# Rotary attention and soft mixture of experts on one core: one normalising product per head pair, and values loaded ahead of weights

## The chip, the cores and the metric

The kernel runs on one core of a Trainium2 chip, in one launch. The metric is the device time in microseconds (us), the median of several runs. The core's engines are TensorE (PE, with its weight loads PEld), VectorE (DVE), ScalarE (ACT), GpSimd (POOL) and SyncE (SP), which here only issues transfers (DMAs).

## The reference

For 8 batches of 8 heads (576 positions, head size 64) queries and keys are rotated, and softmax attention is formed; its result, as 4608 rows of 512, then goes through a soft mixture of 8 experts with 4 slots each.

```python
q_rot, k_rot = (rotate(q), rotate(k))
scores = scale * np.matmul(q_rot, k_rot.transpose(0, 1, 3, 2))
scores = scores - np.max(scores, axis=-1, keepdims=True)
attn = np.exp(scores)
attn = attn / (np.sum(attn, axis=-1, keepdims=True) + 1e-09)
x = (attn @ v) as (B*S, H*D)
logits = x @ phi                       # 4608 x 32
d = softmax of logits over the rows;   slot_input = d.T @ x
slot_out[e] = relu(slot_input[e] @ w1[e]) @ w2[e]
c = softmax of logits over the slots;  out = c @ slot_out
```

## The kernel before

Attention is done for 32 pairs of heads, numbered 0 to 31, four to a batch. For a pair p, queries and keys come in as `x_in` (2 buffers), POOL multiplies them by cosines and sines in eight pieces (`spin0`, `spin1`, L213, called "spins" below), DVE adds the products (`join`, L217), ACT casts the sum to a high half (`high`, L222), and DVE subtracts that half to get the low one (`low`, L226: a subtraction with two inputs in the on-chip memory SBUF, from which POOL reads too). TensorE makes scores once for the row maxima (`m_unit`, L260, reduced on DVE in L262; `m_rem` L269 and L271), then once more from high and low halves with the maxima added (`score`, L313; `score_rest`, L328). The maxima travel from DVE (`m_min` L280, `m_turn` L286) through ACT (`m_half` L290) and five small transfers into `peak` (`m_rows`, L297 and L298). ACT takes the exponentials (L314, L332), and TensorE multiplies them with the values `v_in` (`av`, L344; `load_v`, L232, 2 buffers, so pair p takes the buffer of pair p-2).

`o_out` (ACT, L370 and L372) copies the unnormalised result to `o_sb`: five blocks of 128 positions a head, the fifth with 64 of 128 partitions. `recip` (DVE) adds 1e-9 to the sums, in two instructions L381 and L382, and inverts them (L383); `norm` (POOL) multiplies, in two instructions: L391 on 128 partitions and four blocks, L393 on 64 partitions and the fifth. `natural` (TensorE, L417) transposes the outcome for the logits.

The order of all this is written out by hand: a table gives each step a number (`WHEN`, the same in each pair, and `EARLY` for single steps of single pairs), steps are issued in the order of these numbers, and each engine and SP's queue work through theirs in order. SP's queue waits at its head: a transfer that may not start yet holds all behind it.

The experts' weights (64 tiles `w_exp` of 512 KB) are loaded partly during the last pairs, into space that the input buffers leave free after the last `low`. So that they don't all start at once, the table `PACE` names steps after which one or two such loads stand; each has a one-element memset on DVE ahead (L590), on which the transfer waits, so it can't start before DVE has got that far. The last of them is paced by a one-element copy on POOL instead (L593), which reads the weight tile loaded two earlier. The remaining weights follow when the last pair is done, and stream in while the experts' products (L855, L876) run.

The change touches `PACE`, two numbers of `EARLY` and the functions `o_out`, `recip` and `norm`.

Of the kernel before, what the change touches and what calls it, by code (L numbers as in the profile page):

```python
# [7 lines left out]
F32 = mybir.dt.float32  # L8
# [3 lines left out]
ALU = mybir.AluOpType  # L12
# [21 lines left out]
N_O = 2  # L34
# [15 lines left out]
VW = 66  # L50
N_HL = 3
N_XN = 1
WIDE = True
PACE = {("low", 30): 2, ("recip", 28): 1, ("m_min", 31): 1, ("av0", 30): 1, ("m_rows", 31): 1, ("av0", 31): 1}
WHEN = {
# [70 lines left out]
    30): 122.656032, ("load_v", 30): 122.656033, ("av0", 30): 124.276322, ("norm", 29): 124.926062, ("m_turn",  # L126
# [16 lines left out]
def attn_softmoe(ctx, tc, qk, v, phi, w1, w2, cs, ident, sel, seg, out):  # L143
    nc = tc.nc
    P = 128
# [9 lines left out]
    att = trans.enter_context(tc.tile_pool(name="att", bufs=1))  # L155
# [91 lines left out]
    def free(t):  # L247
        k, _ = held.pop(id(t))
        age[k] = next(ages)
# [86 lines left out]
    os_ = {}  # L336
# [25 lines left out]
    xn_sb = [xp.tile([P, 5, DM], F32, name=f"xn{i}") for i in range(N_XN)]  # L362
    for t in xn_sb:
        nc.gpsimd.memset(t[64:P, 4], 0.0)
    osb = {}

    def o_out(p):
        osb[p] = t = att.tile([P, 2, 5, VW], F32, name="o_sb", bufs=N_O)
        o = os_.pop(p)
        nc.scalar.copy(out=t.rearrange("p h u x -> p h (u x)")[:, :, 0:4 * VW], in_=o[:, :, 0:4 * VW])  # L370
        for h in range(2):
            nc.scalar.copy(out=t[0:64, h, 4], in_=o[rows[h], h, 4 * VW:5 * VW])  # L372
        free(o)

    rrs = [const.tile([P, 2, 5], F32, name=f"rr{i}") for i in range(2)]
    for t in rrs:
        nc.gpsimd.memset(t, 1.0)

    def recip(p):
        rr, t = rrs[p % 2], osb[p]  # L380
        nc.vector.tensor_scalar_add(out=rr[:, :, 0:4], in0=t[:, :, 0:4, 64], scalar1=1e-9)  # L381
        nc.vector.tensor_scalar_add(out=rr[0:64, :, 4], in0=t[0:64, :, 4, 64], scalar1=1e-9)  # L382
        nc.vector.reciprocal(out=rr, in_=rr)  # L383

    def norm(p, eng):
        b, pp = divmod(p, NP)
        if pp == 0:
            xns[b] = xn_sb[b % N_XN]
        xn = xns[b][:, :, pp * P:(pp + 1) * P].rearrange("p j (h x) -> p h j x", h=2)
        t, rr = osb.pop(p), rrs[p % 2]  # L390
        eng.tensor_tensor(out=xn[:, :, 0:4], in0=t[:, :, 0:4, 0:64],  # L391
                          in1=rr[:, :, 0:4].unsqueeze(3).broadcast_to([P, 2, 4, 64]), op=ALU.mult)
        eng.tensor_tensor(out=xn[0:64, :, 4], in0=t[0:64, :, 4, 0:64],  # L393
                          in1=rr[0:64, :, 4].unsqueeze(2).broadcast_to([64, 2, 64]), op=ALU.mult)

    def norm_last(p):
        t = os_.pop(p)
# [207 lines left out]
    def trickle(p, eng=nc.vector):  # L605
        if later:
            load_w(*later.pop(0), pace=eng)
# [135 lines left out]
    for when, n, q in events:  # L743
        run(n, q)
        if n == "low":
            lows.discard(q)
            if not lows and not extra:
                release_io()
        for _ in range(PACE.get((n, q), 0)):
            trickle(last, nc.gpsimd if n == "load_v" else nc.vector)  # L750
# [9 lines left out]
    p = last  # L760
# [21 lines left out]
    m, al, dt, xn = state["m"], state["al"], state["dt"], xns.pop(B - 1)  # L782
# [30 lines left out]
    for i in range(NP):  # L813
# [8 lines left out]
                            in1=e.unsqueeze(1).broadcast_to([P, NP, NS]), op=ALU.mult)  # L822
# [19 lines left out]
    for _ in range(N_LEAD):  # L842
        load_w(wp, N_W)
    nc.vector.tensor_tensor(out=st[:, :, 0:NS], in0=fp[:, 0:P].rearrange("p (c n) -> p c n", c=NP),
                            in1=zw.unsqueeze(1).broadcast_to([P, NP, NS]), op=ALU.mult)
# [166 lines left out]
```

## Time and profile before

| what | value |
|---|---|
| time, median of 3 runs | 524.99 us (521.03, 525.75, 524.99) |
| the profiled execution: its time, and its span | 519.47 us, 517.7 us |
| busy: PE, DVE, ACT, POOL | 473.2, 390.8, 300.8, 296.5 us |
| mean granted TensorE clock | 0.969 of full speed |
| chain that ended last | PE 66%, DVE 25%, issue 3%, DMA 3% |
| one pair of heads, in the middle | about 12 us |
| attention ends, experts begin | about 450 us |
| transfers | 94.03 MB, 182 GB/s in the mean |

The profile shows one execution. Its time and its span differ by 1.8 us, which lie around the instructions. TensorE is busy nearly all the time, so what counts is where it is not, and where its clock falls. The granted clock is given as a share of 2.4 GHz; 0.5 is the lower level, 1.2 GHz. In a list of instructions in order of time, a row has its start, its length, engine, line, operation, what it writes and reads, and in brackets the idle time of the engine ahead of it with what ended it. SPq rows are transfers being issued, not their duration. Several like instructions are merged into a row, with their count after an x.

### The profile page before, as it was taken

How to read it: one execution, taken by the hardware profiler on the slowest of the kernel's cores; microseconds unless marked ns; L12 is line 12 of the kernel's file. 1: busy time of each engine (PE TensorE's matmuls, PEld its weight loads, DVE VectorE, ACT ScalarE, POOL GpSimd, SP SyncE). 2: the span in 40 equal slices, each digit the busy share in tenths (PEclk: the TensorE clock that was granted, in tenths of full speed). 3: DMA queues.
4: the chain of work that ended last, by engine and by line, in shares of the span. 5: the costliest groups of instructions: out<-in, count | busy, mean ns of one | idle time of the engine just before them, and what ended most of it. 6: DMA issues, size and time to landing. Idle time of an engine off the chain costs nothing.

```text
span 517.7 us, 23365 instructions
## 1 busy us (share of the span) xinstructions
PE 473.2 (91%) x10320; PEld 372.5 (72%) x10320; DVE 390.8 (75%) x654; ACT 300.8 (58%) x674; POOL 296.5 (57%) x350
## 2 busy tenths in 40 slices
PE   4499999999999999999999999999969996989990
PEld 2278888787877878787878777878748886843650
DVE  5999988888878887888788878888877851342271
ACT  2156666566666666666766676667637751762551
POOL 2969987577758775867687767728564210220000
PEclk9699999999999999999999999999979997999996
DMA  7267464334544454444444444435322035299998
GB/s 259 92 206 247 165 212 174 124 141 166 217 188 154 161 172 152 163 161 161 162 161 161 162 162 162 161 96 187 120 73 74 5 126 175 91 390 409 395 355 328
DMA packets 29509, 94.03 MB, mean 182 GB/s; under 512 B 5088, under 2 KB 6880, under 8 KB 29408
## 3 DMA queue, kind: packets, MB, share of 16 engines
q1 hardware_dynamic: 29388, 92.54, 49.0%
q8 instruction: 81, 1.33, 1.0%
q14 instruction: 20, 0.16, 0.1%
q10 hardware_dynamic: 20, 0.00, 0.0%
HBM read 83.02 MB, written 9.44 MB: 179 GB/s over the span
## 4 chain that ended last, share of the span: by engine, by line
PE 66%; DVE 25%; issue 3%; DMA 3%; ACT 1%; SPq 0%; POOL 0%; DVEq 0%; ACTq 0%
PE s_ps L313 21%; PE s_ps L344 18%; DVE nm L262 8%; DVE hl L226 6%; PE s_ps L260 5%; DVE x_in L217 5%; PE s_ps L328 4%; PE s_ps L417 4%; PE o_ps L876 3%; PE sp_ps L855 3%; DVE rr L381 2%; PE s_ps L436 2%; PE s_ps L492 1%; DMA out<-w_exp 1%; PE c_ps L902 1%
## 5 line engine op out<-in xcount | busy, mean ns | idle before, releaser
L213 POOL TENSOR_TENSOR x_in<-x_in,cs_sb 128x288 f32<-128x288 f32 x248 | 223.2, 935 | 74.5 <-DMA x_in<-in_qk 73.0
L262 DVE TENSOR_REDUCE nm<-s_ps 128x2 f32<-128x576 f32 x256 | 185.7, 748 | 48.0 <-PE s_ps L260 44.5
L314 ACT ACTIVATE a_t<-s_ps 128x576 f32<-128x576 f32 x256 | 146.7, 655 | 9.8 <-PE s_ps L313 7.9
L344 PE MATMUL s_ps<-v_in,a_t 128*64 128x66 f32 x4608 | 146.8, 224 | 5.7 <-DMA v_in<-in_v 4.4
L344 PEld LDWEIGHTS s_ps<-v_in,a_t 128*64 128x64 f32 x4608 | 141.0, 139 | 15.3 <-issue 7.7
L313 PE MATMUL s_ps<-hl 64*128 64x288 f16 x1536 | 132.0, 284 | 0.0
L313 PEld LDWEIGHTS <-hl 64*128 64x128 f16 x1536 | 78.2, 94 | 17.0 <-issue 2.4
L370 ACT COPY o_sb<-s_ps 128x528 f32<-128x528 f32 x31 | 18.6, 600 | 98.8 <-PE s_ps L344 91.6
L313 PE MATMUL s_ps<-peak,lift 64*128 64x288 f16 x512 | 74.1, 284 | 0.0
L260 PE MATMUL s_ps<-hl 64*128 64x288 f16 x512 | 64.5, 289 | 7.3 <-ACT hl L222 4.1
L222 ACT CAST hl<-x_in 128x576 f16<-128x576 f32 (+1 forms) x66 | 40.9, 655 | 38.6 <-DVE x_in L217 38.5
L391 POOL TENSOR_TENSOR xn<-o_sb,rr 128x512 f32<-128x512 f32 x31 | 41.3, 1331 | 30.2 <-issue 25.1
L226 DVE TENSOR_TENSOR hl<-x_in,hl 128x1152 f16<-128x1152 f32 x32 | 58.0, 1812 | 0.5 <-ACT hl L222 0.5
L217 DVE TENSOR_TENSOR x_in<-x_in 128x1152 f32<-128x1152 f32 (+2 forms) x36 | 51.0, 1419 | 0.4 <-issue 0.3
L260 PEld LDWEIGHTS <-hl 64*128 64x128 f16 x512 | 25.4, 94 | 20.6 <-issue 10.0
L313 PEld LDWEIGHTS <-lift 64*128 64x128 f16 x512 | 25.6, 94 | 6.0
L328 PE MATMUL s_ps<-hl 64*64 64x320 f16 (+1 forms) x384 | 21.7, 292 | 9.0 <-DVE nm L262 8.8
L344 PEld LDWEIGHTS s_ps<-v_in,a_tr 64*64 64x64 f32 x1152 | 21.9, 133 | 10.2 <-issue 10.0
L381 DVE TENSOR_SCALAR rr<-o_sb 128x8 f32<-128x8 f32 x31 | 18.1, 583 | 11.1 <-ACT o_sb L370 11.0
L344 PE MATMUL s_ps<-v_in,a_tr 64*64 64x66 f32 x1152 | 26.4, 224 | 0.0
L271 DVE TENSOR_REDUCE nm<-s_ps 128x2 f32<-128x576 f32 x32 | 23.9, 748 | 2.8 <-PE s_ps L269 2.8
L332 ACT ACTIVATE a_tr<-s_ps 128x512 f32<-128x512 f32 x32 | 19.1, 598 | 10.4 <-PE s_ps L328 9.6
(167 smaller groups left out, 451.2 us busy)
## 6 DMA issues: line engine op xcount, KB each, us to landing
x_in<-in_qk SPq DMA_DIRECT2D x62, 576.0 KB
w_exp<-in_w SPq DMA_DIRECT2D x63, 512.0 KB
v_in<-in_v SPq DMA_DIRECT2D x32, 330.0 KB
out<-w_exp SPq DMA_DIRECT2D x18, 512.0 KB
peak<-mr SPq DMA_DIRECT2D x126, 0.5 KB
x_in<-in_qk SPq DMA_DIRECT2D x4, 288.0 KB
cs_sb<-in_cs SPq DMA_DIRECT2D x2, 288.0 KB
peak<-mr SPq DMA_DIRECT2D x32, 0.2 KB
```

The costliest lines, as they stand in the source:

```text
L213: eng.tensor_tensor(out=x[:, :, c], in0=x[:, :, c], in1=cs_sb[:, :, c], op=ALU.mult)
L217: nc.vector.tensor_tensor(out=x[:, t, 0, c], in0=x[:, t, 0, c], in1=x[:, t, 1, c], op=ALU.add)
L222: nc.scalar.copy(out=halves[p][:, 1 + t, c], in_=loaded[p][:, t, 0, c])
L226: nc.vector.tensor_tensor(out=hl[:, 0:4:3], in0=x[:, :, 0], in1=hl[:, 1:3], op=ALU.subtract)
L260: nc.tensor.matmul(s[c, h, 0:HC], lhsT=hl[rows[h], QH, P * j + c.start:P * j + c.stop], rhs=hl[rows[h], KH, half[n]], start=True, stop=True)
L262: nc.vector.tensor_reduce(out=nm[:, n, j:8:4], in_=s[:, :, 0:HC], axis=AX.X, op=ALU.max, negate=True)
L313: nc.tensor.matmul(s[c, h, 0:HC], lhsT=lhs, rhs=rhs, start=(x == 0), stop=(x == 3))
L314: nc.scalar.activation(out=ats[p, b][:, :, half[n]], in_=s[:, :, 0:HC], func=AF.Exp, scale=SCALE)
L328: nc.tensor.matmul(s[rows[h ^ n], n, 0:w] if n else s[rows[h], 0, 512 - w:512], lhsT=lhs, rhs=rhs, start=(x == 0), stop=(x == 3))
L344: nc.tensor.matmul(o[rows[c], h, VW * u:VW * u + VW], lhsT=lhs, rhs=v, start=(i == 0 and u == first), stop=stop)
L381: nc.vector.tensor_scalar_add(out=rr[:, :, 0:4], in0=t[:, :, 0:4, 64], scalar1=1e-9)
L391: eng.tensor_tensor(out=xn[:, :, 0:4], in0=t[:, :, 0:4, 0:64], in1=rr[:, :, 0:4].unsqueeze(3).broadcast_to([P, 2, 4, 64]), op=ALU.mult)
```

## The change

`o_sb` becomes two fixed tiles, whose lower half of the fifth block (partitions 64 to 127) is set to zero once. `recip` then adds 1e-9 to all ten sums in one instruction, and `norm` is one POOL instruction over 128 partitions and five blocks; the rows that don't exist are products with zero. In the table, `load_v` of pairs 30 and 31 gets smaller numbers, and the weight load that stood after `m_min` of pair 31 now stands after `m_rows` of pair 31, which has two.

```diff
-PACE = {("low", 30): 2, ("recip", 28): 1, ("m_min", 31): 1, ("av0", 30): 1, ("m_rows", 31): 1, ("av0", 31): 1}
+PACE = {("low", 30): 2, ("recip", 28): 1, ("av0", 30): 1, ("m_rows", 31): 2, ("av0", 31): 1}
...
-    30): 122.656032, ("load_v", 30): 122.656033, ("av0", 30): 124.276322, ("norm", 29): 124.926062, ("m_turn",
+    30): 122.656032, ("load_v", 30): 115.540001, ("av0", 30): 124.276322, ("norm", 29): 124.926062, ("m_turn",
...
-    31): 126.278278, ("av1", 30): 126.278280, ("m_rows", 31): 126.373682, ("av4", 30): 127.875064, ("o_out",
+    31): 116.602001, ("av1", 30): 126.278280, ("m_rows", 31): 126.373682, ("av4", 30): 127.875064, ("o_out",
...
-    osb = {}
+    o_sbs = [att.tile([P, 2, 5, VW], F32, name=f"o_sb{i}") for i in range(N_O)]
+    for t in o_sbs:
+        nc.gpsimd.memset(t[64:P, :, 4], 0.0)
...
     rrs = [const.tile([P, 2, 5], F32, name=f"rr{i}") for i in range(2)]
-    for t in rrs:
-        nc.gpsimd.memset(t, 1.0)
...
-        rr, t = rrs[p % 2], osb[p]
-        nc.vector.tensor_scalar_add(out=rr[:, :, 0:4], in0=t[:, :, 0:4, 64], scalar1=1e-9)
-        nc.vector.tensor_scalar_add(out=rr[0:64, :, 4], in0=t[0:64, :, 4, 64], scalar1=1e-9)
+        rr, t = rrs[p % 2], o_sbs[p % N_O]
+        nc.vector.tensor_scalar_add(out=rr, in0=t[:, :, :, 64], scalar1=1e-9)
         nc.vector.reciprocal(out=rr, in_=rr)
...
-        t, rr = osb.pop(p), rrs[p % 2]
-        eng.tensor_tensor(out=xn[:, :, 0:4], in0=t[:, :, 0:4, 0:64],
-                          in1=rr[:, :, 0:4].unsqueeze(3).broadcast_to([P, 2, 4, 64]), op=ALU.mult)
-        eng.tensor_tensor(out=xn[0:64, :, 4], in0=t[0:64, :, 4, 0:64],
-                          in1=rr[0:64, :, 4].unsqueeze(2).broadcast_to([64, 2, 64]), op=ALU.mult)
+        t, rr = o_sbs[p % N_O], rrs[p % 2]
+        eng.tensor_tensor(out=xn, in0=t[:, :, :, 0:64], in1=rr.unsqueeze(3).broadcast_to([P, 2, 5, 64]), op=ALU.mult)
```

SP's queue near the end of attention, from the small transfers of pair 30 (`peak_105`) to those of pair 31 (`peak_106`) and the paced weights (`w_exp`); the two `v_in` are the values of pairs 30 and 31. Before:

```order
L297 DMA peak_105<-mr 2x4x32 x4
L298 DMA peak_105<-mr 2x2x32
L594 DMA w_exp<-in_w 128x1024 x4
L232 DMA v_in<-in_v 128x660
L594 DMA w_exp<-in_w 128x1024
L232 DMA v_in<-in_v 128x660
L297 DMA peak_106<-mr 2x4x32 x4
L298 DMA peak_106<-mr 2x2x32
L594 DMA w_exp<-in_w 128x1024 x2
```

And after:

```order
L297 DMA peak_105<-mr 2x4x32 x4
L298 DMA peak_105<-mr 2x2x32
L232 DMA v_in<-in_v 128x660
L589 DMA w_exp<-in_w 128x1024 x2
L232 DMA v_in<-in_v 128x660
L589 DMA w_exp<-in_w 128x1024 x2
L297 DMA peak_106<-mr 2x4x32 x4
L298 DMA peak_106<-mr 2x2x32
L589 DMA w_exp<-in_w 128x1024 x3
```

The values of pair 30 moved from behind four weights to ahead of all of them, those of pair 31 from behind five to behind two, and one weight from ahead of `peak_106` to behind it.

DVE at the same place: the last reductions of the maxima of pair 31, their minimum (`min_122`) and turn, and the memsets that release paced weights. Before:

```order
L262 TENSOR_REDUCE nm_8890<-s_ps_9261 128x2
L262 TENSOR_REDUCE nm_8890<-s_ps_9286 128x2
L280 TENSOR_REDUCE min_122<-nm_8890 128x9
L590 MEMSET w_exp 1x1 x2
L286 STREAM_TRANSPOSE turned<-min_122 128x32
L590 MEMSET w_exp 1x1
L518 TENSOR_REDUCE cm<-ln 128x5
```

And after:

```order
L262 TENSOR_REDUCE nm_8807<-s_ps_9178 128x2
L262 TENSOR_REDUCE nm_8807<-s_ps_9203 128x2
L280 TENSOR_REDUCE min_122<-nm_8807 128x9
L585 MEMSET w_exp 1x1
L286 STREAM_TRANSPOSE turned<-min_122 128x32
L585 MEMSET w_exp 1x1 x2
L513 TENSOR_REDUCE cm<-ln 128x5
```

One of the two memsets between the minimum and its turn moved behind the turn.

POOL around the normalisation of pair 25, which stands ahead of twelve spins. Before:

```order
L514 TENSOR_TENSOR ln<-ln,cm 128x160
L213 TENSOR_TENSOR x_in<-x_in,cs_sb 128x2x144 x4
L391 TENSOR_TENSOR xn_125<-o_sb,rr_128 128x2x4x64
L393 TENSOR_TENSOR xn_125<-o_sb,rr_128 64x128
L213 TENSOR_TENSOR x_in<-x_in,cs_sb 128x2x144 x12
L391 TENSOR_TENSOR xn_125<-o_sb,rr_127 128x2x4x64
L393 TENSOR_TENSOR xn_125<-o_sb,rr_127 64x128
```

And after:

```order
L509 TENSOR_TENSOR ln<-ln,cm 128x160
L213 TENSOR_TENSOR x_in<-x_in,cs_sb 128x2x144 x4
L389 TENSOR_TENSOR xn_125<-o_sb_128,rr_132 128x2x5x64
L213 TENSOR_TENSOR x_in<-x_in,cs_sb 128x2x144 x12
L389 TENSOR_TENSOR xn_125<-o_sb_127,rr_131 128x2x5x64
```

Of each two products one is left, and the spins that follow stand right behind it. The order on TensorE and ScalarE is the same in both kernels.

## Rows read from the trace of the kernel before

**Rows 1.** Whom TensorE waited for: us in total, times, longest us
```profile
PE s_ps L328 <- DVE nm L262: 8.8, 11, 5.1
...
PE s_ps L344 <- DMA v_in<-in_v: 4.4, 1, 4.4
```

**Rows 2.** SP's queue in order of time, 416 to 432 us: start, us, line
```profile
416.81 11.30 SPq L594 DMA_DIRECT2D w_exp<-in_w  x4
428.20 0.38 SPq L232 DMA_DIRECT2D v_in<-in_v  x1
...
429.63 2.16 SPq L297 DMA_DIRECT2D peak<-mr  x4
431.84 0.51 SPq L298 DMA_DIRECT2D peak<-mr  x1
```

**Rows 3.** The chain that ended last, in order of time: start, us, what
```profile
427.56 0.18 DVE min L280
...
428.20 3.71 DMA v_in<-in_v
...
432.05 7.68 PE s_ps L344 x177
...
444.77 5.12 PE s_ps L344 x180
```

**Rows 4.** Stretches: PE, PEld, DVE, ACT, POOL busy, granted clock, DMA share, GB/s
```profile
371.88:390.39 18.51, 13.41 (x283) 10.79 (x284) 15.58 (x19) 7.90 (x17) 10.47 (x14) 0.82 0.16 52
390.39:402.22 11.83, 11.78 (x287) 10.31 (x286) 8.34 (x15) 8.09 (x19) 5.57 (x6) 1.00 0.27 83
...
432.05:439.00 6.95, 6.95 (x145) 6.88 (x146) 0.00 (x0) 0.00 (x0) 0.00 (x0) 0.60 0.53 186
444.70:449.06 4.36, 4.36 (x146) 4.29 (x144) 1.49 (x5) 2.30 (x6) 0.91 (x2) 1.00 0.18 68
...
456.00:489.00 33.00, 32.52 (x358) 15.52 (x360) 8.98 (x26) 15.59 (x38) 3.99 (x9) 1.00 1.02 405
```

**Rows 5.** DVE in order of time around 373 us
```profile
372.71 0.17 DVE L381 TENSOR_SCALAR rr<-o_sb 128x8 f32<-128x8 f32 x1
...
372.98 0.22 DVE L383 RECIPROCAL rr<-rr 128x10 f32<-128x10 f32 x1
...
374.39 7.58 DVE L226 TENSOR_TENSOR hl<-x_in,hl 128x1152 f16<-128x1152 f32 x1
```

**Rows 6.** POOL in order of time around 373 us
```profile
373.34 1.04 POOL L391 TENSOR_TENSOR xn<-o_sb,rr 128x512 f32<-128x512 f32 x1 [2.83 <-DVE rr L383]
374.35 0.40 POOL L393 TENSOR_TENSOR xn<-o_sb,rr 64x128 f32<-64x128 f32 x1
374.70 6.05 POOL L213 TENSOR_TENSOR x_in<-x_in,cs_sb 128x288 f32<-128x288 f32 x8
```

**Rows 7.** All instructions of line 226: ns least/median/most, first and last start
```profile
L226 DVE TENSOR_TENSOR hl<-x_in,hl x32: 1317/1578/7583, 11.7 to 415.0; 128x1152 f16<-128x1152 f32 x32
```

**Rows 8.** DVE and POOL in order of time in two other pairs
```profile
113.85 1.57 DVE L226 TENSOR_TENSOR hl<-x_in,hl 128x1152 f16<-128x1152 f32 x1
...
113.80 0.40 POOL L393 TENSOR_TENSOR xn<-o_sb,rr 64x128 f32<-64x128 f32 x1
...
322.86 2.20 DVE L226 TENSOR_TENSOR hl<-x_in,hl 128x1152 f16<-128x1152 f32 x1
...
322.80 1.04 POOL L391 TENSOR_TENSOR xn<-o_sb,rr 128x512 f32<-128x512 f32 x1
323.80 1.51 POOL L393 TENSOR_TENSOR xn<-o_sb,rr 64x128 f32<-64x128 f32 x1
```

**Rows 9.** ACT and POOL in order of time, pair 31's maxima and the paced copy
```profile
428.33 0.23 ACT L290 ACTIVATE mr<-turned 128x32 f16<-128x32 f32 x1
...
442.61 0.18 POOL L593 COPY w_exp<-w_exp 1x1 f32<-1x1 f32 x1
448.15 0.46 POOL L521 TENSOR_TENSOR cn_sb<-ln,cm 128x160 f32<-128x160 f32 x1 [5.37 <-DVE cm L520]
```

More of the change, by code (lines that the diff above doesn't have):

```diff
@@ L364, in attn_softmoe @@
         nc.gpsimd.memset(t[64:P, 4], 0.0)
-    osb = {}
+    o_sbs = [att.tile([P, 2, 5, VW], F32, name=f"o_sb{i}") for i in range(N_O)]
+    for t in o_sbs:
+        nc.gpsimd.memset(t[64:P, :, 4], 0.0)
     def o_out(p):
-        osb[p] = t = att.tile([P, 2, 5, VW], F32, name="o_sb", bufs=N_O)
-        o = os_.pop(p)
+        t, o = o_sbs[p % N_O], os_.pop(p)
         nc.scalar.copy(out=t.rearrange("p h u x -> p h (u x)")[:, :, 0:4 * VW], in_=o[:, :, 0:4 * VW])
```

## The prediction

> **What bounds the kernel now.** I read first whom TensorE waits for, since it is busy nearly all the time. Two waits stand out: 4.4 us once, at the product with the values (L344), for the transfer of `v_in`, and 5.1 us once within the 8.8 us that L328 waits for DVE's reductions; the other ten of these share 3.7 us [rows 1]. Then I looked at the place of each.
>
> The wait for the values lies in pair 30. SP's queue holds four weight transfers from 416.81 to 428.11, and only then, at 428.20, issues `v_in` [rows 2]. The fourth weight waits for a memset that stands on DVE behind the minimum of pair 31, which ends at 427.74; the chain goes from that minimum to the transfer of the values, 3.71 us, and from its landing to 177 matmuls of L344 that take 7.68 us, where pair 31's 180 take 5.12 us [rows 3]. The reader is to see that values needed at about 427.7, when the last scores of pair 30 end, were queued behind a weight that nobody needs before the experts begin. The matmuls are slower because the granted clock in 432 to 439 us is 0.60, and 1.00 in the same work of pair 31 (6.95 us against 4.36) [rows 4]: after the pause most of it runs at 1.2 GHz.
>
> The wait for DVE lies at 377 to 383 us. There one `low` (L226) takes 7.58 us from 374.39 on [rows 5], where the median of 32 is 1.58 [rows 7]. All that time POOL works without a gap: L391, L393, then eight spins until 380.75 [rows 6], and L226 ends 1.2 us after the last spin, about its own least length of 1.32 [rows 7]. So DVE stood aside for eight POOL instructions in a row. TensorE's pair there takes 18.51 us at a clock of 0.82, the next pair, with the same work, 11.83 at 1.00 [rows 4].
>
> Behind 450 us the DMA engines are full (share 1.02, 405 GB/s, from 456 to 489 us [rows 4]) with TensorE busy beside them; both streams start when the last pair ends, so this part moves as a whole with that end.
>
> **The change part by part.**
>
> *Values ahead of weights.* Pair 30's values now wait only for their buffer, that of pair 28, and stand directly behind the small transfers of pair 30, ahead of the weight issued at 416.81 [rows 2]: they are issued at about 416.8 and by the 3.71 us of [rows 3] are there at 420.5, seven us before use. Pair 31's wait for the buffer of pair 29, whose products end before the last scores of pair 30; they were needed at 444.77 [rows 3], and that becomes 437.9: not on the path either way. The weights behind them wait for memsets that DVE reaches no later than before. What goes is the pause, 427.70 to 432.05, and the slow clock behind it, 7.68 - 5.12 = 2.56 us [rows 3]: 4.35 + 2.56 = 6.9 us.
>
> What is late next? `score_rest` of pair 31 needs its maxima, whose transfers were issued from 429.63 to 432.35 [rows 2], behind the values. ACT has their data ready at 428.56 [rows 9], so now they go out from about 428.6 to 431.3. TensorE finishes pair 30's products at 427.7 + 5.1 = 432.8 and needs the maxima within the step after that. If a small transfer lands within 2 us of its issue, nothing waits; if the last, issued at 430.8, takes the 3.71 us of the values, it lands at 434.5 and up to 1.7 us come back. I take none: these transfers are a small fraction of the values' size, and only one weight is under way ahead of them. So 5.2 to 6.9 us, 6.9 taken.
>
> *One product on POOL.* L391 (512 elements) takes 1.04 us, L393 (128) 0.40, and together they run from 373.34 to 374.75, 1.41 us [rows 6]. The slope between them is 0.64/384 = 1.7 ns an element, so 640 take 1.04 + 128 x 0.0017 = 1.26 us; bounds are 1.04 and 1.44, the sum of the two. POOL saves about 0.15 us a pair, worth nothing by itself, since the list of waits names none of TensorE for POOL; without that cover it would be 31 x 0.15 = 4.7 us. Where DVE arrives within it, it may wait up to 0.22 us longer.
>
> *One addition on DVE.* L381 ends at 372.88 and L383 starts at 372.98, 0.10 us later, for the L382 between them [rows 5]. That is what a pair can gain on DVE, and it shows on TensorE only in the ten pairs that wait for DVE at L328, 0.37 us each [rows 1]: 10 x 0.10 = 1.0 us. Bounds are a gain of 3.7, all these waits, and a loss of 2.2, if each of the ten meets the longer product and waits 0.22 more. I take 1.0.
>
> *The long wait of L226.* It starts while L393 runs (374.35 to 374.75), and POOL's next instruction is ready [rows 6]. In another pair L226 also met L393, but with nothing behind it on POOL, and took 1.57; in a third it met L391, with L393 ready behind, and there DVE went first: L393 stretched to 1.51 and L226 took 2.20 [rows 8]. So a `low` that arrives in a 128-partition instruction goes next, and the one case with a 64-partition instruction in progress and more behind it lost eight times. The change takes the 64-partition instruction away. L226 now arrives at about 374.3, L389 runs from 373.3 to 374.5, and L226 should run then, for some 1.6 us. It would end at about 375.9 in place of 381.97 [rows 5], 6.1 us earlier, more than the 5.1 that TensorE waited [rows 1]; so the wait goes, and the slow clock after it, 18.51 - 11.83 = 6.7 us together [rows 4]. It is one case in 32, so the bounds are wide: 0 if the cause is another, 6.7 if it is this; I take 6.7, as the row nearest to it, the third pair's, has DVE going first.
>
> The Trainium skill (SBUF — State Buffer, Who interferes with whom) says that whichever of the two engines issues first holds the shared ports for its whole instruction, and that the order of issue and not the shape decides who blocks. The trace agrees for L391 and L393 in the third pair [rows 8], but not at 374 us, where eight spins that came after L226 went ahead of it [rows 6]. By the letter of that rule the product's shape would not matter, and a wait like this would be as likely as before; that is the first rival below.
>
> *Sum* against the profiled execution's 519.47 us: 519.47 - 6.9 - 6.7 - 1.0 = 504.9. That execution lies 1.6 us under the fastest and 5.5 under the median of the runs shown (521.03 to 525.75). These runs differ among themselves by 4.7 us, nearly the price of one long wait of L226, so they may well hold one more of these, and lose it too; if the 5.5 are something else, the median would be 510.4. I take a point between, nearer the first: 507.
>
> **The rivals.**
>
> 1. *The values help, DVE's long wait stays.* The cause is not the 64 partitions but spins that stand ready behind one another; then some pair still meets it. For it: the spins behind L391 and L393 are eight in a row, and one case is little evidence. Against: the third pair of [rows 8], and that half of all `low`s take 1.58 or less [rows 7]. Time: 504.9 + 6.7 = 511.6 in an execution like the profiled one, and 5.5 more, 517.1, by the median. The rule of the Trainium skill named above speaks for this one.
>
> 2. *The wait for the values comes back as another.* The maxima of pair 31 are late, or POOL's paced copy is. That copy reads a weight that is now issued behind the maxima, at about 431.4; by size that is 3.71 x 512/330 = 5.8 us, so at worst it lands at 437.2. Moved up by 6.9, the copy was due at 435.7 (442.61 before), and POOL's next work, on which pair 30's product and the end of attention hang, at 441.2 (448.15 before) [rows 9]: four us to spare. So it costs at most 1.7 us, from the maxima, unless transfers take about twice as long as that; then up to all 6.9 return: 511.8, and 517.3 by the median.
>
> 3. *Slower.* The single product puts spins directly behind each normalisation, and if a `low` that arrives in it loses as at 374 us, this happens in more pairs. Each costs 6.7 us. One such wait is there now; two give 504.9 + 13.4 = 518.3, three 525.0, four 531.7: from four on the kernel is slower in an execution like the profiled one, from three on (530.5) by the median. Against it: with a 128-partition product in progress DVE went first [rows 8].
>
> **How the numbers follow.** Both gains: 0.67, 503 to 511, point 507. Rival 1: 0.20, 512 to 517. Rival 2: 0.06, about 507 to 517. Rival 3: 0.07, half of it with two or three waits (518 to 526), half beyond. The likeliest case's own range is 503 to 511; the whole range, 503 to 517, takes in rivals 1 and 2 and leaves out rival 3 and the tails, about 0.15. A measurement of this kernel can tell about 1% (5.2 us) from no change, so faster means under 519.7 and slower over 530.2: faster 0.89, no change 0.07, slower 0.04.
>
> **What would show it.** The wait of L344 for `v_in` is gone from the list of waits, L344 of pair 30 takes 5.1 us, and the granted clock from 428 us on stays at 1.00; SP issues both values before 422 us and `peak` for pair 31 from about 428.6 (less what was gained earlier). If TensorE waits at L328 for `peak`, the step on what is late next is wrong. L226 has no length above about 2.4 us, and L389 takes 1.2 to 1.4 us; one `low` of over 4 us shows rival 1, several rival 3. L381 and L382 shrink to one instruction, with L328's other waits at 2.7 us in place of 3.7. If the part behind the last pair is not as long as before (about 68 us), its DMA stream was not bound to that end.

## The result and the profile after

| | before | after |
|---|---|---|
| median | 524.67 us (521.03 to 525.75, 4 runs) | 505.39 us (504.54 to 506.79, 4 runs) |
| ratio, 95% interval | | 0.964 (0.960 to 0.969) |
| profiled execution: time, span | 519.47, 517.7 us | 504.54, 502.7 us |
| granted TensorE clock, mean | 0.969 | 0.981 |
| busy: PE, DVE, ACT, POOL | 473.2, 390.8, 300.8, 296.5 us | 467.7, 380.1, 301.1, 287.2 us |

The changed kernel is 3.6% faster. The ratios in this text leave out one run as slow, that of 511.32 us of `e10_drain` below, since it lies over 1.5% above the fastest of its kernel. Lines of after are a few numbers lower: L389 is the one product (L391 and L393 before), L380 the one addition, L589 the weights, L412 the transposes.

Whom TensorE waited for, after (us in total, times, longest); it answers [rows 1]:

```profile
PE s_ps L328 <- DVE nm L262: 2.9, 5, 1.0
PE s_ps L412 <- POOL xn L389: 2.1, 5, 0.9
PE s_ps L260 <- DVE nm L262: 2.1, 5, 0.9
```

The 4.4 us for `v_in` and the one wait of 5.1 us for DVE are gone. A new line stands there: five waits for the single POOL product, 2.1 us. Two longer ones that [rows 1] does not show, for ACT in the first 22 us, are as they were: 6.9 and 4.1 us before, 7.0 and 4.0 after.

SP's queue, after, against [rows 2]:

```profile
408.90 0.52 SPq L298 DMA_DIRECT2D peak<-mr  x1
409.51 0.33 SPq L232 DMA_DIRECT2D v_in<-in_v  x1
409.96 1.20 SPq L589 DMA_DIRECT2D w_exp<-in_w  x2
414.21 0.33 SPq L232 DMA_DIRECT2D v_in<-in_v  x1
414.74 6.08 SPq L589 DMA_DIRECT2D w_exp<-in_w  x2
421.30 2.15 SPq L297 DMA_DIRECT2D peak<-mr  x4
```

The values of pair 30 go out at 409.51, 10.8 us before their use at 420.34; the maxima of pair 31 at 421.30, as soon as ACT has them (L290 starts at 421.04). The chain that ended last, after, against [rows 3]: the products of pair 30 take 5.03 us, those of pair 31 5.12 as before, and no transfer stands between.

```profile
420.41 5.03 PE s_ps L344 x177
426.41 4.06 PE s_ps L313 x64
430.47 5.12 PE s_ps L344 x180
```

The stretches that answer [rows 4] (PE, PEld, DVE, ACT, POOL busy, granted clock, DMA share, GB/s): about pair 26, about pair 27, the products of pair 30, and 33 us of the experts.

```profile
371.60:383.35 11.75, 11.74 (x287) 10.28 (x287) 9.65 (x16) 7.79 (x19) 9.81 (x11) 1.00 0.24 82
383.35:395.10 11.75, 11.70 (x287) 10.21 (x287) 8.71 (x16) 8.01 (x19) 7.06 (x8) 1.00 0.27 83
420.41:425.44 5.03, 5.03 (x186) 4.96 (x190) 0.94 (x8) 1.09 (x4) 0.46 (x1) 1.00 0.39 120
...
441.50:474.50 33.00, 32.52 (x356) 15.60 (x358) 8.97 (x25) 15.38 (x38) 3.93 (x9) 1.00 1.02 405
```

Pair 26 took 18.51 us at a clock of 0.82; by the starts in the table below it now takes 11.59, at 1.00. Pair 30's products run at 1.00 where 0.60 was granted. The place of the long `low`, DVE and POOL in order of time, and all instructions of L226, against [rows 5 to 7]:

```profile
374.12 1.43 DVE L226 TENSOR_TENSOR hl<-x_in,hl 128x1152 f16<-128x1152 f32 x1
...
373.07 1.26 POOL L389 TENSOR_TENSOR xn<-o_sb,rr 128x640 f32<-128x640 f32 x1 [2.81 <-DVE rr L381]
374.29 7.19 POOL L213 TENSOR_TENSOR x_in<-x_in,cs_sb 128x288 f32<-128x288 f32 x8
```
```profile
L226 DVE TENSOR_TENSOR hl<-x_in,hl x32: 1317/1352/2475, 12.0 to 407.7; 128x1152 f16<-128x1152 f32 x32
```

`low` arrives while L389 runs, with eight spins ready behind, and goes next: 1.43 us in place of 7.58.

Where the 14.9 us between the two profiled executions lie, by the starts of the products L344 of each pair:

| start of L344 of pair | before | after | earlier by | added since the row above |
|---|---|---|---|---|
| 26 | 371.88 | 371.67 | 0.21 | 0.2, twenty-six pairs |
| 27 | 390.39 | 383.26 | 7.13 | 6.9, the long `low` |
| 29 | 415.71 | 408.42 | 7.29 | 0.2 |
| 30 | 432.05 | 420.34 | 11.71 | 4.4, the wait for `v_in` |
| 31 | 444.70 | 430.41 | 14.29 | 2.6, the clock behind it |
| end of the execution | 519.47 | 504.54 | 14.93 | 0.6 |

### The profile page after: what moved, and what is told of

It is laid out like the page before. It is cut to its first block, busy times and chain, and to the rows that moved or that the text cites. A ratio compares the mean times of both kernels' runs of the same rounds, so it can differ in the third digit from the quotient of the medians.

```text
span 502.7 us, 23304 instructions
## 1 busy us (share of the span) xinstructions
PE 467.7 (93%) x10320; PEld 369.5 (74%) x10320; DVE 380.1 (76%) x623; ACT 301.1 (60%) x674; POOL 287.2 (57%) x319
## 3 DMA queue, kind: packets, MB, share of 16 engines
q8 instruction: 81, 1.33, 1.1%
## 4 chain that ended last, share of the span: by engine, by line
PE 57%; DVE 17%; POOL 11%; DMA 7%; issue 3%; ACT 2%; SPq 1%; POOLq 0%; DVEq 0%; ACTq 0%
PE s_ps L313 18%; PE s_ps L344 16%; POOL x_in L213 9%; DMA x_in<-in_qk 6%; DVE x_in L217 5%; PE s_ps L260 5%; DVE nm L262 4%; PE s_ps L412 3%; PE o_ps L871 3%; PE sp_ps L850 3%; DVE hl L226 3%; PE s_ps L328 2%; POOL xn L389 2%; PE s_ps L431 2%; DVE rr L380 2%
## 5 line engine op out<-in xcount | busy, mean ns | idle before, releaser
L213 POOL TENSOR_TENSOR x_in<-x_in,cs_sb 128x288 f32<-128x288 f32 x248 | 231.5, 968 | 76.5 <-DMA x_in<-in_qk 66.8
L344 PEld LDWEIGHTS s_ps<-v_in,a_t 128*64 128x64 f32 x4608 | 138.6, 137 | 10.7 <-ACT a_t L314 6.5
L344 PE MATMUL s_ps<-v_in,a_t 128*64 128x66 f32 x4608 | 144.4, 222 | 0.9 <-issue 0.3
L389 POOL TENSOR_TENSOR xn<-o_sb,rr 128x640 f32<-128x640 f32 x31 | 41.3, 1334 | 27.6 <-issue 14.2
L217 DVE TENSOR_TENSOR x_in<-x_in 128x1152 f32<-128x1152 f32 (+2 forms) x36 | 53.4, 1487 | 0.9 <-POOL x_in L213 0.7
L226 DVE TENSOR_TENSOR hl<-x_in,hl 128x1152 f16<-128x1152 f32 x32 | 47.9, 1497 | 0.5 <-ACT hl L222 0.5
L344 PEld LDWEIGHTS s_ps<-v_in,a_tr 64*64 64x64 f32 x1152 | 22.0, 133 | 10.2 <-issue 10.0
L344 PE MATMUL s_ps<-v_in,a_tr 64*64 64x66 f32 x1152 | 26.5, 224 | 0.0
L412 PE MATMUL s_ps<-id_sb,xn 128*128 128x128 f32 x160 | 23.4, 280 | 2.5 <-POOL xn L389 2.1
L328 PE MATMUL s_ps<-hl 64*64 64x320 f16 (+1 forms) x384 | 21.4, 287 | 4.1 <-DVE nm L262 2.9
L412 PEld LDWEIGHTS s_ps<-id_sb,xn 128*128 128x128 f32 x160 | 17.0, 141 | 10.6 <-POOL xn L389 7.2
```

Of the source, the lines that this page charges most:

```text
L213: eng.tensor_tensor(out=x[:, :, c], in0=x[:, :, c], in1=cs_sb[:, :, c], op=ALU.mult)
L217: nc.vector.tensor_tensor(out=x[:, t, 0, c], in0=x[:, t, 0, c], in1=x[:, t, 1, c], op=ALU.add)
L226: nc.vector.tensor_tensor(out=hl[:, 0:4:3], in0=x[:, :, 0], in1=hl[:, 1:3], op=ALU.subtract)
L328: nc.tensor.matmul(s[rows[h ^ n], n, 0:w] if n else s[rows[h], 0, 512 - w:512], lhsT=lhs, rhs=rhs, start=(x == 0), stop=(x == 3))
L344: nc.tensor.matmul(o[rows[c], h, VW * u:VW * u + VW], lhsT=lhs, rhs=v, start=(i == 0 and u == first), stop=stop)
L389: eng.tensor_tensor(out=xn, in0=t[:, :, :, 0:64], in1=rr.unsqueeze(3).broadcast_to([P, 2, 5, 64]), op=ALU.mult)
```

## The experiments

My theory after the result: three of the steps are real and separate (the values, the clock, the 64 partitions), and the unexplained 5.5 us between the profiled execution and the median of before are a second long wait of DVE. Its rivals: the normalisation's gain comes from having fewer POOL instructions, or from the moved work; and the long wait comes from spins that stand ready behind each other, whatever their shapes.

**The two halves alone.** `e1_values` is the kernel before with the order of transfers only:

```diff
-PACE = {("low", 30): 2, ("recip", 28): 1, ("m_min", 31): 1, ("av0", 30): 1, ("m_rows", 31): 1, ("av0", 31): 1}
+PACE = {("low", 30): 2, ("recip", 28): 1, ("av0", 30): 1, ("m_rows", 31): 2, ("av0", 31): 1}
...
-    30): 122.656032, ("load_v", 30): 122.656033, ("av0", 30): 124.276322, ("norm", 29): 124.926062, ("m_turn",
+    30): 122.656032, ("load_v", 30): 115.540001, ("av0", 30): 124.276322, ("norm", 29): 124.926062, ("m_turn",
...
-    31): 126.278278, ("av1", 30): 126.278280, ("m_rows", 31): 126.373682, ("av4", 30): 127.875064, ("o_out",
+    31): 116.602001, ("av1", 30): 126.278280, ("m_rows", 31): 126.373682, ("av4", 30): 127.875064, ("o_out",
```

> Only the order of transfers is changed (values of pairs 30 and 31 ahead of the weights, one weight moved behind the maxima); the two POOL products and the two additions stay. Theory: the wait of TensorE for v_in (4.4 us) and the slow clock behind it go, 6.9 us, and nothing else; the long wait of one L226 (over 4 us) stays in the profile, at about the same pair. In an execution like the profiled one of the kernel before: 519.5 - 6.9 = 512.6, by the median of its runs about 517.8, ratio 0.987. Rival (the values' wait comes back as one for the maxima of pair 31): under 3 us gained, and L328 waits for peak. Rival (one order change does it all): about 505.

Measured: 517.77 us beside 524.26 for the kernel before, ratio 0.983 (0.977 to 0.990). The wait for `v_in` is gone. DVE's long wait stays, and there are two of them:

```profile
379.49 7.58 DVE L226 TENSOR_TENSOR hl<-x_in,hl 128x1152 f16<-128x1152 f32 x1
...
58.88 5.95 DVE L217 TENSOR_TENSOR x_in<-x_in 128x1152 f32<-128x1152 f32 x1
```

`e2_norm` is the kernel before with the other half: the zeroed lower half of `o_sb`, one addition, one product.

```diff
-        nc.vector.tensor_scalar_add(out=rr[:, :, 0:4], in0=t[:, :, 0:4, 64], scalar1=1e-9)
-        nc.vector.tensor_scalar_add(out=rr[0:64, :, 4], in0=t[0:64, :, 4, 64], scalar1=1e-9)
+        nc.vector.tensor_scalar_add(out=rr, in0=t[:, :, :, 64], scalar1=1e-9)
...
+        eng.tensor_tensor(out=xn, in0=t[:, :, :, 0:64], in1=rr.unsqueeze(3).broadcast_to([P, 2, 5, 64]), op=ALU.mult)
```

> Only the normalisation is changed (one addition on DVE, one POOL product over 128 partitions, zeroed o_sb); the order of transfers is that of the kernel before. Theory (the long wait of L226 comes from the 64-partition product): no L226 over 3 us, the wait for v_in stays at about 4.4 us; 519.5 - 6.9 = 512.6 in an execution like the profiled one, and if the runs of the kernel before hold more long waits than its profile does, more than that by the median, 512 to 514 against 524.7, ratio 0.977 to 0.981. Rival (the long wait has another cause and was absent by chance from the changed kernel's profile): one L226 over 4 us in the profile, or runs that differ among themselves by 4 us or more.

Measured: 511.97 us beside the same 524.26, ratio 0.975 (0.968 to 0.981). Its four runs lie 6.4 us apart (508.05 to 514.48), which I had named as a sign of the rival, that the long wait is absent by chance. The one that was profiled (513.52 us) does not bear the rival out: no L226 or L217 over 2.1 us; TensorE waits for the values:

```profile
PE s_ps L344 <- DMA v_in<-in_v: 4.8, 1, 4.8
```

So each half brings its own gain, and within the noise they add: 6.5 + 12.3 = 18.8 us of the medians, each known to some 3 us, where both together brought 19.3. The normalisation is worth more than the 6.7 + 1.0 that the one profiled execution of before showed; the second long wait, which this execution of `e1_values` has too, is a candidate for the rest.

**A second execution of the kernel before.** `e4_before_again` is the kernel before, unchanged.

> The kernel before, unchanged, profiled once more. Theory (the long wait of L226 is a matter of arrival times, so executions hold different numbers of it, which makes the spread of 521 to 525.8 us): the profile holds one to three L226 of over 4 us, and its time over 519.5 is about 6.7 us for each beyond the first, less where TensorE does not need the result at once. Rival (the 5 us between profiled execution and median are something else): one long L226 at the same pair and a time of 521 to 526 all the same.

Measured: 524.0 us. Its long `low` is there as in [rows 5] (7.58 us at 378.40), and this beside it:

```profile
57.55 6.13 DVE L217 TENSOR_TENSOR x_in<-x_in 128x1152 f32<-128x1152 f32 x1
...
56.03 0.40 POOL L393 TENSOR_TENSOR xn<-o_sb,rr 64x128 f32<-64x128 f32 x1
56.39 6.08 POOL L213 TENSOR_TENSOR x_in<-x_in,cs_sb 128x288 f32<-128x288 f32 x8
```

In the execution that the prediction started from, the same place read:

```profile
57.56 1.88 DVE L217 TENSOR_TENSOR x_in<-x_in 128x1152 f32<-128x1152 f32 x1
...
56.04 0.39 POOL L393 TENSOR_TENSOR xn<-o_sb,rr 64x128 f32<-64x128 f32 x1
56.68 8.31 POOL L213 TENSOR_TENSOR x_in<-x_in,cs_sb 128x288 f32<-128x288 f32 x8 [0.25 <-DMA x_in<-in_qk]
```

The difference is POOL's pause of 0.25 us between L393 and the first spin, for a transfer of `x_in`. Without it, the `join` of DVE, which arrives 1.1 us after L393 has ended, waits for six spins. From pair 2 to pair 3 the second execution falls 3.8 us behind the first, and it ends 4.5 behind, most of what lay between the first and the median. It also corrects the theory: the 64-partition product need not be in progress when DVE comes. Here it had ended, and POOL had not paused since.

**Shape or number.** Three kernels take the changed kernel and cut its product in two along the blocks, as before: both pieces over 128 partitions (`e3_split128`, and `e3_again` with the changed kernel, `after_again`, beside it), or the second over 64 (`e5_split64`).

```diff
-        eng.tensor_tensor(out=xn, in0=t[:, :, :, 0:64], in1=rr.unsqueeze(3).broadcast_to([P, 2, 5, 64]), op=ALU.mult)
+        eng.tensor_tensor(out=xn[:, :, 0:4], in0=t[:, :, 0:4, 0:64],
+                          in1=rr[:, :, 0:4].unsqueeze(3).broadcast_to([P, 2, 4, 64]), op=ALU.mult)
+        eng.tensor_tensor(out=xn[:, :, 4], in0=t[:, :, 4, 0:64],
+                          in1=rr[:, :, 4].unsqueeze(2).broadcast_to([P, 2, 64]), op=ALU.mult)
```

In `e5_split64` the second piece reads instead:

```diff
+        eng.tensor_tensor(out=xn[0:64, :, 4], in0=t[0:64, :, 4, 0:64],
+                          in1=rr[0:64, :, 4].unsqueeze(2).broadcast_to([64, 2, 64]), op=ALU.mult)
```

> The changed kernel with its POOL product cut in two again, four blocks and the fifth, but both over 128 partitions. Theory (64 partitions are the cause): no L226 over 3 us, time within 1 us of the changed kernel's 505.4. Rival (a short product with spins ready behind it is the cause, whatever its partitions): one or more L226 over 4 us, at the pair where L226 arrives within the second product, and 505.4 + 6.7 = 512. Also, TensorE's waits for the POOL product at the transposes (2.1 us in the changed kernel) tell whether one longer product is the reason: they should shrink to under 1 us if it is.

> The changed kernel, unchanged, beside the split one on the same chip. Theory (the time between runs of it is only noise of loads, with no long wait): median 505 to 506.5, no L226 or L217 over 3 us in the profile.

> Two POOL products over 128 partitions each, as in the run that cut the product in two, once more beside the changed kernel. Theory (one longer product makes the transposes of TensorE wait, 2.1 us in the changed kernel's profile, and the shorter first one does not): 1 to 3 us faster than the changed kernel of the same call, 502.5 to 504.5. Rival (the difference of 2.9 us between the two was one of sessions): within 1 us of it, and the POOL waits of TensorE the same in both profiles.

> The changed kernel with the POOL product cut in two as in the kernel before: four blocks over 128 partitions, the fifth over 64; everything else, the single addition on DVE too, as changed. It differs from the two products over 128 partitions by these 64 partitions alone. Theory (a 64-partition product leaves DVE without its turn until POOL's unbroken run ends): one or two two-input DVE instructions over 5 us, one at pair 25 or so and in some runs one at pair 3, 505.4 + 6.7 to 505.4 + 10.7 = 512 to 516. Rival (number or length of the products): no such wait and 503 to 506.

Measured: `e3_split128` 502.5 us, ratio 0.959 (0.954 to 0.964); and, measured later, `after_again` 506.48, 0.966 (0.963 to 0.970), `e3_again` 505.56, 0.964 (0.960 to 0.968), and `e5_split64` 514.36, 0.982 (0.978 to 0.986). Two products instead of one cost nothing. Sixty-four partitions in the second cost 8.8 us against `e3_again`, the same instructions otherwise, and the place is the known one:

```profile
374.71 7.58 DVE L226 TENSOR_TENSOR hl<-x_in,hl 128x1152 f16<-128x1152 f32 x1
...
374.67 0.40 POOL L391 TENSOR_TENSOR xn<-o_sb,rr 64x128 f32<-64x128 f32 x1
375.03 6.04 POOL L213 TENSOR_TENSOR x_in<-x_in,cs_sb 128x288 f32<-128x288 f32 x8
```

In `e3_again`, at the same place, DVE arrives in the same product over 128 partitions and goes next:

```profile
372.34 1.57 DVE L226 TENSOR_TENSOR hl<-x_in,hl 128x1152 f16<-128x1152 f32 x1
...
372.30 0.40 POOL L391 TENSOR_TENSOR xn<-o_sb,rr 128x128 f32<-128x128 f32 x1
372.66 7.18 POOL L213 TENSOR_TENSOR x_in<-x_in,cs_sb 128x288 f32<-128x288 f32 x8
```

So the shape is the cause, not the number of instructions. One place speaks against a simple rule: at 58.26 us of `e5_split64` a `join` arrived 1.1 us after a 64-partition product in an unbroken run of POOL, and took 1.63 us. There the transfer that the first spin behind the product waits for landed 0.10 us after the product had started. Where DVE lost in the kernels with a 64-partition product, that wait had ended before the product started, by 0.2 us or more.

Whether the split over 128 partitions beats the changed kernel stays open. I had expected 1 to 3 us of `e3_again`; measured side by side, the medians lie 0.9 us apart and the intervals overlap. TensorE's waits for the product are 0.5 us in `e3_split128`, 1.3 in `e3_again` and 1.6 in `after_again`.

**64 partitions without a follower.** `e7_halves` cuts the changed kernel's product by partitions, 0 to 63 and 64 to 127:

```diff
-        eng.tensor_tensor(out=xn, in0=t[:, :, :, 0:64], in1=rr.unsqueeze(3).broadcast_to([P, 2, 5, 64]), op=ALU.mult)
+        for c in rows:
+            eng.tensor_tensor(out=xn[c], in0=t[c, :, :, 0:64], in1=rr[c].unsqueeze(3).broadcast_to([64, 2, 5, 64]), op=ALU.mult)
```

> The changed kernel with the POOL product cut by partitions, 0 to 63 and 64 to 127, five blocks each, so two 64-partition instructions of the full length stand in each pair. Theory: every subtraction or sum of DVE that arrives in an unbroken run of POOL with one of them in it waits to the end of the run; some six or more of these of 3 us or more in place of none, and the time over 520. Rival (only a short product does it, or chance): none or one, and about 511 at most, from the longer work on POOL.

Measured, one run: 527.51 us, but no L226 or L217 over 2.1 us: all long waits that I expected were missing, and the time came out over 520 for another reason. Each half takes as long as the whole (1.26 us), and TensorE waits for them:

```profile
PE s_ps L413 <- POOL xn L390: 20.7, 16, 2.5
```

In this kernel POOL stands idle for 74 to 76 ns between the halves (58 in one pair) and for 78 or more behind them. Between them it waits for its own instruction. That suggested that such a pause lets DVE in. `e10_drain` tests it: `e5_split64` and one copy of a column that the 64-partition product wrote, so that POOL must wait for that product.

```diff
         eng.tensor_tensor(out=xn[0:64, :, 4], in0=t[0:64, :, 4, 0:64],
                           in1=rr[0:64, :, 4].unsqueeze(2).broadcast_to([64, 2, 64]), op=ALU.mult)
+        eng.tensor_copy(out=drained, in_=xn[:, 0, 4, 0:1])
```

> The changed kernel with the second normalising product on 64 partitions again (as in e5_split64, which took 514 us), plus one POOL copy of one column behind it that reads what this product wrote, so that POOL waits for its own product before it goes on to the spins. The work is otherwise the same. Theory (DVE loses a whole run only if a 64-partition instruction is followed by ready ones without a gap): POOL pauses some 75 ns behind the product, DVE's subtraction gets in, no L226 or L217 over 2.6 us, 504.5 to 508 us. Rival (the 64-partition product by itself, however followed, makes DVE wait, or the reduced idle time around it): again one L226 of 5 us or more, 511 to 515 us.

Measured: 503.85 us, ratio 0.963 (0.955 to 0.971), clear of `e5_split64`'s 0.982 (0.978 to 0.986): an instruction more, and some ten us less. One of its four runs took 511.32 us, though, 7 us more than the other three, at a mean clock of 0.967 in place of 0.978 to 0.980; it has no trace, so a long wait in it is not ruled out. In the profiled run 63 or 64 ns lie between product and copy in all 31 pairs, and no L226 or L217 is over 2.3 us. At the known place:

```profile
372.90 1.57 DVE L226 TENSOR_TENSOR hl<-x_in,hl 128x1152 f16<-128x1152 f32 x1
...
372.86 0.39 POOL L393 TENSOR_TENSOR xn<-o_sb,rr 64x128 f32<-64x128 f32 x1
373.32 1.20 POOL L395 COPY drained<-xn 128x1 f32<-128x1 f32 x1
```

DVE arrived in the 64-partition product, as in [rows 5, 6], and went ahead of the copy. That the copy runs over 128 partitions is not the reason, since the spins right behind the product in `e5_split64` do so too, and DVE waited for eight of them.

**The dose.** If the theory holds, more 64-partition instructions must make it worse. `e11_dose64` and `e12_dose128` add to the changed kernel one small product on scratch space behind the first of each four spins, over 64 and over 128 partitions (62 of them, two a pair, 0.28 us each; the first expectation has four of 0.15):

```diff
         for i, c in enumerate(cols):
             ...
+            if i == 0 and eng is nc.gpsimd:
+                eng.tensor_tensor(out=dose[0:64, t], in0=id_sb[0:64, 0:48], in1=id_sb[0:64, 48:96], op=ALU.mult)
```

> The changed kernel with one small extra POOL product (48 elements a partition, on scratch space, not part of the computation) behind the first of each four spins, over 64 partitions. Theory (a 64-partition instruction with ready ones behind it shuts DVE out to the end of the unbroken run): now many pairs have one, so in several pairs L226 or the join arrives in such a run and waits for all of it: at least four instructions of over 3.5 us, and some 5 to 40 us above the changed kernel, 511 to 545 us. Rival (the long waits before came from the place of the normalising product and its run of eight spins, not from the 64 partitions): no more long ones than with 128 partitions, 506 to 511 us (about 0.15 us more POOL work four times a pair, under cover).

> As e11_dose64, but the small extra product runs over 128 partitions. Theory: at most one POOL instruction passes a waiting DVE instruction, so no L226 or join over 2.6 us, and 505 to 511 us. Rival (more and shorter POOL instructions in a row shut DVE out, whatever their partitions): several L226 or joins of over 3.5 us here too, and about the time of e11_dose64.

Measured, one run each: 572.97 us with 64 partitions, 505.07 with 128. All instructions of `join` (L221 here) and `low` (L230), ns least/median/most, with 64 first:

```profile
L221 DVE TENSOR_TENSOR x_in<-x_in x36: 457/3118/8127, 5.8 to 463.2; 128x1152 f32<-128x1152 f32 x30, 128x288 f32<-128x288 f32 x4, 128x576 f32<-128x576 f32 x2
...
L230 DVE TENSOR_TENSOR hl<-x_in,hl x32: 1298/1426/7529, 11.3 to 476.1; 128x1152 f16<-128x1152 f32 x32
```
```profile
L221 DVE TENSOR_TENSOR x_in<-x_in x36: 457/1408/1956, 6.0 to 395.4; 128x1152 f32<-128x1152 f32 x30, 128x288 f32<-128x288 f32 x4, 128x576 f32<-128x576 f32 x2
...
L230 DVE TENSOR_TENSOR hl<-x_in,hl x32: 1297/1389/2014, 11.9 to 408.2; 128x1152 f16<-128x1152 f32 x32
```

The clearest rows are near the start, where DVE arrives at 17.89 us in both. With 64 partitions, then with 128:

```profile
17.89 8.13 DVE L221 TENSOR_TENSOR x_in<-x_in 128x576 f32<-128x576 f32 x1
...
16.41 0.28 POOL L217 TENSOR_TENSOR dose<-id_sb 64x48 f32<-64x48 f32 x1
16.66 3.02 POOL L215 TENSOR_TENSOR x_in<-x_in,cs_sb 128x288 f32<-128x288 f32 x4
19.65 0.28 POOL L217 TENSOR_TENSOR dose<-id_sb 64x48 f32<-64x48 f32 x1
19.89 3.03 POOL L215 TENSOR_TENSOR x_in<-x_in,cs_sb 128x288 f32<-128x288 f32 x4
22.88 0.28 POOL L217 TENSOR_TENSOR dose<-id_sb 64x48 f32<-64x48 f32 x1
23.12 2.28 POOL L215 TENSOR_TENSOR x_in<-x_in,cs_sb 128x288 f32<-128x288 f32 x3
```
```profile
17.89 0.92 DVE L221 TENSOR_TENSOR x_in<-x_in 128x576 f32<-128x576 f32 x1
...
16.41 0.28 POOL L217 TENSOR_TENSOR dose<-id_sb 128x48 f32<-128x48 f32 x1
16.65 3.55 POOL L215 TENSOR_TENSOR x_in<-x_in,cs_sb 128x288 f32<-128x288 f32 x4
```

The same addition of DVE lets eleven POOL instructions pass in the one, and goes next in the other. With 64 partitions 21 instructions take over 3.5 us, and the sum of all time over 1.5 us in L221 and L230 is 78.8 us, against 6.2 with 128; the difference, 72.6, is near that of the two times, 67.9. My expectation had the direction right and the size too small (511 to 545).

Now all the traces together. An unbroken run of POOL is one with pauses under 30 ns; counted is each `join` or `low` that arrived in a POOL instruction with another ready behind it.

- In the seven traces without a 64-partition instruction in POOL's runs (two of the changed kernel, both of `e3`, `e2_norm`, `e8_pace_only`, `e12_dose128`) there are 296 such arrivals: 250 times DVE went next, 46 times one POOL instruction passed first, never two.
- Where the unbroken run up to the arrival held a 64-partition instruction, 32 of 35 waited to the end of the run: 26 of 27 in `e11_dose64`, 6 of 8 in the two traces of before, `e1_values` and `e5_split64`. In four of the 32 only one instruction was left in the run, so these four fit either rule.
- Two of the three exceptions are pair 3 of `e5_split64`, told above (the second follows the first in the same run). In the third, at 241.44 us of `e11_dose64`, POOL gave way after one, ahead of a spin that waits for the other half of `x_in`; by the trace this transfer landed at 242.42 us, so the spin was not ready when DVE came.

In both places a spin became ready only while the instruction ahead of it ran, 0.2 to 0.3 us before that one ended. That this lets DVE in as a pause does is a guess. At 38.39 us of `e11_dose64` a spin became ready 0.55 us before the end of the one ahead, and DVE waited to the end of the run all the same.

**Which edit moved the values.** `e8_pace_only` puts the numbers of `load_v` back and leaves only the one weight moved:

```diff
-    30): 122.656032, ("load_v", 30): 115.540001, ("av0", 30): 124.276322, ("norm", 29): 124.926062, ("m_turn",
+    30): 122.656032, ("load_v", 30): 122.656033, ("av0", 30): 124.276322, ("norm", 29): 124.926062, ("m_turn",
...
-    31): 116.602001, ("av1", 30): 126.278280, ("m_rows", 31): 126.373682, ("av4", 30): 127.875064, ("o_out",
+    31): 126.278278, ("av1", 30): 126.278280, ("m_rows", 31): 126.373682, ("av4", 30): 127.875064, ("o_out",
```

> The changed kernel with the numbers of load_v of pairs 30 and 31 put back; only the weight that stood ahead of the last maxima stays moved behind them. SP's queue then reads: three weights, values of pair 30, one weight, values of pair 31, the maxima of pair 31, three weights. Theory (it was the one weight whose memset stands behind the minimum of pair 31 that held the values; their own place in the queue matters little): the values of pair 30 now stand behind a weight whose memset follows the sums of pair 28, are issued about 6 us ahead of the minimum of pair 31 and land before use; no wait of TensorE for v_in, and the time of the changed kernel, 504 to 508 us. Rival (the place of load_v is what brings the gain): the pause of 4.4 us and the slow clock behind it, 2.6 us, come back at the products of pair 30, 511 to 515 us.

Measured: 506.31 us, ratio 0.968 (0.962 to 0.973), as the changed kernel. No wait for `v_in`; SP's queue:

```profile
410.74 5.54 SPq L589 DMA_DIRECT2D w_exp<-in_w  x3
416.38 0.39 SPq L232 DMA_DIRECT2D v_in<-in_v  x1
421.70 0.33 SPq L589 DMA_DIRECT2D w_exp<-in_w  x1
```

The values stand behind three weights and still leave at 416.38, some 5 us ahead of the minimum of pair 31 (421.47). Only the fourth weight, which waits for that minimum, had held them. The other half of the edit, the values moved ahead and the weight left where it was, was not run.

## Why the prediction was right, step by step

**Values ahead of weights: right, to a tenth.** 6.9 us predicted; 4.4 + 2.6 = 7.0 in the table of starts. What should show it did: L344 of pair 30 at 5.03 us, clock 1.00. The step named the held queue rightly, but credited the place of `load_v`; `e8_pace_only` shows that taking the one weight out of the way is enough, and that the new numbers of `load_v` beside it add nothing that can be measured. Whether they would have been enough alone is open. *What is late next*: nothing. TensorE never waits for `peak`, the paced copy moved with the rest (428.32 against 442.61 in [rows 9]), so the bound of 1.7 us came to 0.

**The long wait of L226: right in size, and the cause held.** 6.7 predicted, 6.9 found. The cause as put, a 64-partition instruction in progress with work behind, was too narrow: it may have ended 1.1 us earlier (`e4_before_again`), and several instructions back (`e11_dose64`), as long as POOL has not paused since, with three exceptions in 35. That the single case of [rows 5, 6] pointed to the right cause is what the experiments show; the case alone did not. Rival 1, that spins ready behind each other are enough, fell with `e12_dose128` and the 296 arrivals. Its rule, of the Trainium skill (SBUF — State Buffer, Who interferes with whom), that the order of issue and not the shape decides who is blocked, does not hold here: `e11_dose64` and `e12_dose128` differ in shape alone, 573 against 505 us, and eleven later POOL instructions passed the waiting one.

**One product on POOL: the size right, "worth nothing" not borne out.** L389 takes 1.26 us alone, as estimated. The cover that I claimed came from the list of waits of a single execution. TensorE waits for the product 2.1 us in the profiled execution of after, 1.6 and 1.7 in `after_again` and `e8_pace_only`, 0.8 in `e2_norm`. With two products it is nothing in [rows 1], but 0.5 in the second execution of before, and 0.5 to 1.3 in both of `e3` and in `e5_split64`. So neither is fully covered, and whether the single product costs a microsecond more is not shown.

**One addition on DVE: mis-sized.** 1.0 us was taken. L328's other waits fell from 3.7 to 2.9 us between the two profiled executions, but the second one of before has 3.1 and the second one of the changed kernel 4.5, so that this fall is the addition's is not shown. The steady pairs gained only 0.4 us in all (the rows of pairs 26 and 29 in the table). Both executions wander by over 1 us in this part against each other (earlier by 1.33 at pair 12, later by 0.12 at pair 19), so the term is lost in that.

**Sum and median.** 504.9 forecast for the profiled execution, 504.54 found: the errors (values 0.1 and long wait 0.2 too small, addition 0.6 too large, the part behind the last pair 0.6 shorter) nearly cancel. From the end of attention to the end of the span it was 67.8 us and is 67.1, with the DMA share at 1.02 and 405 GB/s in both, as [rows 4] had it. The 5.5 us to the median were guessed to be one more long wait that goes too; `e4_before_again` and `e1_values` show such a wait, at pair 3. That guess set the point at 507 and not at 510; the rest of before's spread was not looked into.

## What to carry to other kernels

A transfer that waits for a late step holds all behind it in its queue: look first for the one entry whose release comes last, and move that one. Where DVE shares SBUF with a busy GpSimd, give GpSimd's instructions all 128 partitions, even if half of the work is on zeros, or, on the weaker evidence of `e10_drain`, make GpSimd wait for itself behind a narrow one. One rare long instruction in a list of 32 is worth a look at what its neighbour engine did just then. And before costing a change on one profiled execution, ask what the other executions have that it lacks.

## What the runs showed of the hardware

- A POOL product costs the same over 64 as over 128 partitions: 0.28 us for 48 elements either way, 1.26 for 640.
- A DVE instruction with two inputs in SBUF that arrives in an unbroken run of POOL with a 64-partition instruction in it waits to the end of that run, in 32 of 35 arrivals: up to eleven instructions and 8.13 us. Where all are over 128 partitions, one at most passes it. A pause of 63 ns behind the narrow one undid it in the trace of `e10_drain`. Narrow instructions in such runs were all on partitions 0 to 63; no others were tried.
- Why, no trace shows. The Trainium skill (GPSIMD Engine Reference, Instruction dispatch) says that the cores of GpSimd serve 16 partitions each, that a core goes on to the next instruction as soon as its own share is done, and that nothing holds the cores together but what an instruction itself does, so that where it matters a wait for completion has to stand between two. That would fit: after a 64-partition instruction half of the cores run ahead, so one or the other half is always reading, until a wait brings them together. It is argued, not shown.
- Where DVE goes first, a spin is stretched: of 248 spins 37 take over 0.9 us in `e12_dose128`, up to 2.0, and 4 in `e11_dose64`, where DVE waits. The means are 956 and 805 ns, the medians 796 and 789.
